# Output products of a gated linear recurrence: one layout against another, ahead of a folded feed-forward part on one Trainium2 core

## The chip, the cores and the metric

The kernel runs on one core of one Trainium2 chip. The metric is device time in microseconds of that core for one execution, the median over several runs. Engines are named as the profile names them: PE is TensorE (PEld its weight loads), DVE is VectorE, ACT is ScalarE, POOL is GpSimd, SP is the engine that issues most DMAs.

## What is computed

The reference has two parts. A recurrence with a state per batch and head, decayed per feature by alpha, is read by q at each step; then a feed-forward part takes, element by element, the largest of three products, and multiplies it by a last matrix.

```
B, H, S, D = 4, 8, 768, 48
for t in range(S):
    state = alpha[:, :, t, :, None] * state + einsum('bhd,bhe->bhde', k[:, :, t], v[:, :, t])
    y[:, :, t] = einsum('bhd,bhde->bhe', q[:, :, t], state)
x = y.transpose(0, 2, 1, 3).reshape(B * S, H * D)          # 3072 x 384
h = maximum(maximum(x @ w1, x @ w2), x @ w3)               # 3072 x 768
out = h @ w_out                                            # 3072 x 384, float32
```

## The kernel before

Tokens are cut into 24 units: 6 blocks of 128 steps (cb) times 4 batches (b), unit u = 4 cb + b. Within a unit the recurrence is written as products. ACT takes the logarithm of alpha (L398), PE sums it along time with a triangular matrix (`cums`, L438), and ACT makes the two exponentials `ep` and `en` (L443, L446). DVE or POOL multiplies them into q and k (L450). The values v are scaled on POOL or ACT with a factor per row, `vsc` (L457, L460), into tiles of 384 columns, one stretch of 48 per head. The scaled q and k are turned by PE and copied out (L479, L486), or, for the units in `CROSS_Q`, turned by a DMA. Then `scores` (L495) makes for each of 8 heads a 128 x 128 product of k and q; these use 48 rows, two heads of a pair in the upper and the lower half of the array. DVE masks them into `LA` (L500).

`output(u)` makes the unit's outputs. In `outs` (L538, L541) the stationary operands are the turned q of a head pair (against the state Z of that pair, 96 columns) and the masked scores LA of one head (against 48 columns of v). The result has steps in partitions and features in columns. `left` copies it out of PSUM into `xb` with the factor per row `ysc` that takes back the scaling of v (L552 on ACT, L554 on DVE). Since the feed-forward part needs features in partitions, `turn` (L568) turns `xb` with 3 PE transposes and a second copy makes `xT` (L573); for the three units in `CROSS_X` a DMA turns it instead (L561). Units 0 to 3 have no state yet, so their `outs` has only the 8 products with v.

`state(u)` makes the next state: PE's `sums` (L600), DVE's addition `U` (L607), and two multiplications by the decay G on POOL or DVE (`Z`, L613). The state tiles hold 4 pairs of 96 columns.

`ffn` takes one unit at a time (the first four and the last two) or two. In `grow` (L638) it multiplies xT by the differences w2 - w1 and w3 - w1, in `relu` and `max` (L649, L654) it takes the largest with zero, and in `shrink` (L674) it multiplies this by w_out and adds xT times the product w1 w_out, which `turned` and `folded` make once (L362, L379). `ob` copies the result out (L689), and `store` writes it.

The order of all work is written out by hand: every piece is a step with a number, `ORDER` lists the numbers in the order in which they are issued to their engines, `BANKS` gives each PSUM result one of 8 banks, and `PICK` names the steps that take the second of their engines. The durations in `plan.step` are those by which the order was once made; at run time they do nothing. `warm` puts 27 products of zeros (L582) into PE's stream in the first stage.

The setup clears parts of tiles: `la`, `qk` and all of Z, on DVE (L274, L276, L279).

Of the kernel before, what the change touches and what calls it, by code (L numbers as in the profile page):

```python
# [16 lines left out]
CDEC = 0.92  # L17
SIG = 128.0

# [9 lines left out]
CROSS_X = (16, 20, 22)  # L29
# [50 lines left out]
)  # L80
BANKS = (
# [9 lines left out]
)  # L91
PICK = {
# [8 lines left out]
}  # L101

# [68 lines left out]
def kernel(  # L171
# [103 lines left out]
    for t in qks[:QKS]:  # L275
        nc.vector.memset(t[:, :, :, D:], 0.0)  # L276
# [486 lines left out]
```

## Time and profile before

| | |
|---|---|
| median of three runs | 153.33 us |
| lowest and highest run | 152.72 and 155.74 us |
| span of the profiled execution | 466.5 us |
| PE busy in it | 457.5 us |
| DVE, ACT, POOL busy | 112.5, 90.1, 48.0 us |
| read from memory, written | 23.69 MB, 4.72 MB |

The profiled execution has no time of its own beside its span; the span runs from the first to the last instruction. It is three times the median of the timed runs, so a number of the trace can't be carried over to them without a look at what in it is slow; the prediction does that first.

How to read the lines: the head of the page gives each engine's busy time, its share of the span and its number of instructions. A line of the groups names the line of the kernel, the engine, the operation, output and inputs, their shapes and the number of instructions; then busy time and the mean duration of one in ns; then the idle time of the engine ahead of them and who ended it. A line of the timeline gives start and duration in us, then the same names; neighbours of one kind are merged, and x6 is their number. The duration of a matmul is modelled, its start is recorded, so distances between starts are the safer measure.

### The profile page before, as it was taken

What the parts mean: (1) busy time and instruction counts of PE and PEld (TensorE: products, weight loads), DVE (VectorE), ACT (ScalarE), POOL (GpSimd) and SP (SyncE); (2) the same over time, 40 slices, a digit from 0 to 9 for tenths busy, and PEclk for the clock granted to TensorE, in tenths of its full rate; (3) what the DMA queues carried; (4) which work ended last, traced back from release to release, by engine and by line L of the source; (5) the groups of instructions that cost most, each with busy time, mean ns of one, the idle gap of its engine ahead of it and who ended that gap; (6) DMA issues with size and microseconds to landing.
All of it is one profiled execution on the core that took longest, in us unless ns stands there. A gap on an engine that the chain in (4) does not pass through costs nothing.

```text
span 466.5 us, 4171 instructions
## 1 busy us (share of the span) xinstructions
PE 457.5 (98%) x1683; PEld 263.5 (56%) x1683; DVE 112.5 (24%) x196; ACT 90.1 (19%) x177; POOL 48.0 (10%) x72
## 2 busy tenths in 40 slices
PE   4999999999999999999999999999999999999997
PEld 1667556674555656547546645545546554567473
DVE  5420313131123122222412221322221321231100
ACT  4323221122121312111212200121220111001010
POOL 0110002003001030210111120011110020000000
DMA  9999500540087000700032640020550030100001
GB/s 179 272 287 209 110 0 1 111 76 1 0 163 124 1 0 18 152 17 35 0 60 49 141 91 9 2 62 0 112 112 17 18 79 25 35 0 25 1 34 34
DMA packets 116131, 31.07 MB, mean 67 GB/s; under 512 B 109712, under 2 KB 114960, under 8 KB 116112
## 3 DMA queue, kind: packets, MB, share of 16 engines
q1 hardware_dynamic: 113232, 27.27, 27.9%
q10 hardware_dynamic: 2880, 3.54, 2.2%
q8 instruction: 13, 0.21, 0.2%
q14 instruction: 6, 0.05, 0.0%
HBM read 23.69 MB, written 4.72 MB: 61 GB/s over the span
## 4 chain that ended last, share of the span: by engine, by line
PE 98%; DMA 1%; SPq 0%; DVE 0%; issue 0%; DVEq 0%
PE psum L638 38%; PE psum L674 29%; PE psum L479 6%; PE psum L495 4%; PE psum L582 4%; PE psum L541 3%; PE psum L438 3%; PE psum L568 3%; PE psum L600 3%; PE psum L538 2%; PE psum L379 2%; DMA qn<-in_q_dram 1%; PE psum L362 1%; PE psum L408 1%; SPq L304 0%; DVE qk L450 0%
## 5 line engine op out<-in xcount | busy, mean ns | idle before, releaser
L638 PE MATMUL psum<-xT,wd 128*128 128x256 f16 (+1 forms) x540 | 186.4, 602 | 0.0
L638 PEld LDWEIGHTS <-wd 128*128 128x128 f16 x540 | 105.1, 209 | 67.5 <-issue 61.5
L674 PE MATMUL psum<-wo,hT 128*128 128x384 f16 (+1 forms) x150 | 96.7, 887 | 0.0
L674 PEld LDWEIGHTS <-hT 128*128 128x128 f16 x150 | 34.4, 230 | 54.6 <-issue 52.0
L674 PE MATMUL psum<-w1o,xT 128*128 128x384 f16 (+1 forms) x75 | 50.1, 847 | 0.0
L654 DVE TENSOR_TENSOR hT<-psum,hT 128x512 f16<-128x512 f32 (+1 forms) x39 | 24.7, 647 | 99.7 <-PE psum L638 99.7
L649 ACT ACTIVATE hT<-psum 128x512 f16<-128x512 f32 (+1 forms) x39 | 21.7, 564 | 111.0 <-PE psum L638 111.0
L500 DVE TENSOR_TENSOR LA<-psum,c 128x1024 f16<-128x1024 f32 x24 | 28.9, 1221 | 41.0 <-PE psum L495 28.7
L541 PE MATMUL psum<-v,LA 128*128 128x48 f16 x192 | 30.3, 314 | 0.0
L541 PEld LDWEIGHTS <-LA 128*128 128x128 f16 x192 | 26.5, 179 | 5.7 <-issue 5.1
L613 POOL TENSOR_TENSOR Z<-U,G 48x192 f16<-48x192 f32 x26 | 14.1, 543 | 109.5 <-DVE U L607 108.5
L438 PE MATMUL psum<-la,c 128*128 128x384 f16 x24 | 19.9, 847 | 4.3 <-ACT la L398 4.3
L479 PE MATMUL psum<-c,qk 128*128 128x128 f16 x96 | 22.1, 480 | 1.7 <-DVE qk L450 1.7
L479 PEld LDWEIGHTS <-qk 128*128 128x128 f16 x96 | 16.9, 208 | 9.1 <-DVE qk L450 4.0
L450 POOL TENSOR_TENSOR qk<-qn,ep 128x384 f16<-128x384 f32 x11 | 10.9, 994 | 105.2 <-ACT ep L443 94.0
L674 PEld LDWEIGHTS <-xT 128*128 128x128 f16 x75 | 13.1, 185 | 14.7 <-issue 14.2
L582 PE MATMUL psum<-Z 128*128 128x384 f16 x27 | 20.2, 869 | 0.0
L443 ACT ACTIVATE ep<-psum 128x384 f32<-128x384 f32 x24 | 11.7, 494 | 41.3 <-PE psum L438 41.2
L689 ACT COPY ob<-psum 128x384 f32<-128x384 f32 (+1 forms) x18 | 8.3, 469 | 54.7 <-PE psum L674 54.7
L554 DVE TENSOR_SCALAR xb<-psum,c 128x384 f16<-128x384 f32 x15 | 9.2, 617 | 37.9 <-PE psum L541 37.9
L568 PE MATMUL psum<-c,xb 128*128 128x128 f16 x63 | 17.5, 455 | 0.0
L446 ACT ACTIVATE en<-psum 128x384 f32<-128x384 f32 x24 | 11.5, 490 | 28.4 <-PE psum L438 27.1
(61 smaller groups left out, 297.2 us busy)
## 6 DMA issues: line engine op xcount, KB each, us to landing
out_dram<-ob ACTq DMA_DIRECT2D x17, 192.0 KB, 1.9
an<-in_alpha_dram SPq DMA_DIRECT2D x8, 384.0 KB, 5.3
kn<-in_k_dram SPq DMA_DIRECT2D x8, 384.0 KB, 5.4
qn<-in_q_dram SPq DMA_DIRECT2D x8, 384.0 KB, 5.7
vn<-in_v_dram SPq DMA_DIRECT2D x8, 384.0 KB, 4.2
ws<-in_moe_w_dram SPq DMA_DIRECT2D x3, 768.0 KB, 6.7
an<-in_alpha_dram SPq DMA_DIRECT2D x8, 192.0 KB, 4.0
kn<-in_k_dram SPq DMA_DIRECT2D x8, 192.0 KB, 4.0
```

The costliest lines, as they stand in the source:

```text
L438: nc.tensor.matmul(live[Lk], tri, la[:, hs, :D], start=True, stop=True)
L479: nc.tensor.transpose(live[tk][:, w, j, :], qk[:, w, 2 * j:2 * j + 2, :], ident)
L495: nc.tensor.matmul(live[Ak][:, p, j * P:(j + 1) * P], qkT[rows, 1, j, :], qkT[rows, 0, j, :], start=True, stop=True)
L500: lambda e: nc.vector.tensor_mul(LA.rearrange("p a b t -> p (a b) t"), live[Ak].rearrange("p a (b t) -> p (a b) t", t=P), maskA.unsqueeze( ...
L541: nc.tensor.matmul(yp[:, 2 * j + p, :], LA[:, p, j, :], v16[:, 2 * j + p, :], start=(cb == 0), stop=True, skip_group_check=True)
L568: nc.tensor.transpose(live[xk][:, ft, :], xb[:, ft * P:(ft + 1) * P], ident)
L582: nc.tensor.matmul(live["wm"], zero[:, :P], zero, start=True, stop=True)
L613: lambda e, rows=rows, cols=cols: engines[e].tensor_mul(Zn[rows, :, cols], (Us[u % 3] if cb else live[pk])[rows, :, cols], G[rows, i * NP: ...
L638: nc.tensor.matmul(live[gk][:, jj, :], wd[:, kt, g, j * P:(j + 1) * P], xT[:, kt, :], start=(kt == 0), stop=(kt == NFT - 1))
L649: lambda e, h=h, gk=gk: nc.scalar.activation(out=h, in_=live[gk], func=AFT.Relu),
L654: lambda e, h=h, gk=gk: nc.vector.tensor_max(h, live[gk], h),
L674: nc.tensor.matmul(live[ok][:, cols], a[:, i * P:(i + 1) * P], w[:, cols], start=(kt == 0), stop=(kt == nk - 1))
```

## The change

The 64 features of each half of a 128-feature block of xT are now made directly, features in partitions and steps in columns. Values and state become the stationary operands, 64 columns of them at a time, and LA and the turned q the moving ones, 128 columns each. Heads are 48 wide, so a 64-feature half takes columns of two neighbouring heads; that a head adds nothing to its neighbour's features, v is stored twice as wide (768 columns), even heads in the first 384 and odd heads in the second, zeros elsewhere, and the state likewise in tiles of 512 columns, with pairs 0 and 2 at one offset and 1 and 3 at another. The two halves of a block go to PSUM partitions 0 to 63 and 64 to 127 of the same columns, and their products are issued alternately. `xb`, its turn, the second copy and the three DMA turns are gone; the first copy writes xT, with the constant factor 1/16. The factor per row moves to `ob`, where steps are in partitions again. `ORDER` is the old one without the steps that are gone, with the steps `xT` where `xb` stood; `BANKS` and `PICK` follow. The v tiles are cleared on POOL at the start.

```
+XS = 1.0 / 16.0
-CROSS_X = (16, 20, 22)
+    ZP = P + HALF // 2
-        [SIG / dec, dec / SIG, np.full(P, HALF * np.log(CDEC))], axis=1
+        [SIG / dec, dec / SIG / XS, np.full(P, HALF * np.log(CDEC))], axis=1
-    v16s = homes(7, [P, H, D], FP16, "v")
+    v16s = homes(7, [P, 2 * DM], FP16, "v")
-    Zs = [homes(B, [P, NP, 2 * D], FP16, f"Z{i}_") for i in range(2)]
+    Zs = [homes(B, [P, NP * P], FP16, f"Z{i}_") for i in range(2)]
+    def heads_of(t):
+        return bass.AP(t.tensor, t.offset, [t.ap[0], [DM + D, 2], [2 * D, NP], [1, D]])
+    def pairs_of(t):
+        return bass.AP(t.tensor, t.offset, [t.ap[0], [2 * P, NP // 2], [ZP, 2], [1, 2 * D]])
+    for t in v16s:
+        nc.gpsimd.memset(t, 0.0)
+        def terms(g):
+            lo, hi = g * HALF, (g + 1) * HALF
+            out = []
+            if cb > 0:
+                for j in range(NP):
+                    if 2 * D * j < hi and 2 * D * (j + 1) > lo:
+                        at = (j // 2) * 2 * P + (j % 2) * ZP + lo - 2 * D * j
+                        out.append((Z[:, at:at + HALF], qkT[:, 0, j, :]))
+            for h in range(H):
+                if D * h < hi and D * (h + 1) > lo:
+                    at = (h % 2) * DM + lo
+                    out.append((v16[:, at:at + HALF], LA[:, h % 2, h // 2, :]))
+            return out
         def outs(e):
-            yp = live[yk] = bank(yk, [P, H, D], FP32)
-            for j in range(NP):
-                if cb > 0:
-                    nc.tensor.matmul(yp[:, 2 * j:2 * j + 2, :], qkT[:, 0, j, :], Z[:, j, :], ...)
-                for p in range(2):
-                    nc.tensor.matmul(yp[:, 2 * j + p, :], LA[:, p, j, :], v16[:, 2 * j + p, :], ...)
+            yp = live[yk] = bank(yk, [P, NFT, P], FP32)
+            for i in range(NFT):
+                both = [terms(2 * i), terms(2 * i + 1)]
+                for k in range(max(map(len, both))):
+                    for w in range(2):
+                        if k < len(both[w]):
+                            lhsT, rhs = both[w][k]
+                            nc.tensor.matmul(yp[w * HALF:(w + 1) * HALF, i, :], lhsT, rhs,
+                                             start=(k == 0), stop=(k == len(both[w]) - 1),
+                                             skip_group_check=True)
         def left(e):
-            (ACT or DVE) xb = y * ysc
+            (ACT or DVE) xT = live[yk] * XS
-        def turn(e): ...
-        plan.step(f"x turn {u}", ...), plan.step(f"xT {u}", ...)
...
-                              nc.scalar.copy if e == "ACT" else nc.vector.tensor_copy)(
-                                  out=ob, in_=live[ok][:, cols]),
+                              nc.scalar.activation(out=ob, in_=live[ok][:, cols], func=AFT.Copy,
+                                                   scale=ysc) if e == "ACT" else
+                              nc.vector.tensor_scalar(out=ob, in0=live[ok][:, cols], scalar1=ysc,
+                                                      scalar2=None, op0=AOP.mult)),
```

The writes of v, and the reads and writes of the state in `U`, `Z` and `sums`, go through `heads_of` and `pairs_of`; their number of elements is the same.

More of the change, by code (lines that the diff above doesn't have):

```diff
@@ L239 @@
     qks = homes(QKS, [P, 2, H, DP], FP16, "qk")
-    v16s = homes(7, [P, H, D], FP16, "v")
+    v16s = homes(7, [P, 2 * DM], FP16, "v")
     qkTs = homes(QKTS, [P, 2, NP, P], FP16, "qkT")
     LAs = homes(3, [P, 2, NP, P], FP16, "LA")
-    xbs = homes(5, [P, DM], FP16, "xb")
     xTs = homes(NX, [P, NFT, B * P], FP16, "xT")
@@ L453, in prep @@
                       writes=[("qk", hq[u], w)])
+        vin = ld["v"][n % LOADED][:, hs].rearrange("p (m y) d -> p y m d", y=2)
         def scaled(e):
             if e == "ACT":
-                nc.scalar.activation(out=v16, in_=ld["v"][n % LOADED][:, hs], func=AFT.Copy,
-                                     scale=vsc)
-            else:
-                nc.gpsimd.tensor_scalar(out=v16, in0=ld["v"][n % LOADED][:, hs], scalar1=vsc,
-                                        scalar2=1.0, op0=AOP.mult, op1=AOP.mult)
+                nc.scalar.activation(out=heads_of(v16), in_=vin, func=AFT.Copy, scale=vsc)
+            else:
+                nc.gpsimd.tensor_scalar(out=heads_of(v16), in0=vin, scalar1=vsc, scalar2=1.0,
+                                        op0=AOP.mult, op1=AOP.mult)
         plan.step(f"v {u}", [("POOL", 0.59), ("ACT", 0.62)], u, scaled,
@@ L528, in output @@
         cb, b = divmod(u, B)
-        qkT, LA, v16, xb = qkTs[ht[u]], LAs[u % 3], v16s[u % 7], xbs[u % 5]
+        qkT, LA, v16 = qkTs[ht[u]], LAs[u % 3], v16s[u % 7]
         Z = Zs[cb % 2][b]
-        yk, xk = ("yp", u), ("xp", u)
+        yk = ("yp", u)
         xT = xTs[cb % NX][:, :, b * P:(b + 1) * P]
-        def outs(e):
-            yp = live[yk] = bank(yk, [P, H, D], FP32)
-            for j in range(NP):
-                if cb > 0:
-                    nc.tensor.matmul(yp[:, 2 * j:2 * j + 2, :], qkT[:, 0, j, :], Z[:, j, :],
-                                     start=True, stop=False, skip_group_check=True)
-                for p in range(2):
-                    nc.tensor.matmul(yp[:, 2 * j + p, :], LA[:, p, j, :], v16[:, 2 * j + p, :],
-                                     start=(cb == 0), stop=True, skip_group_check=True)
-        plan.step(f"outs {u}", [("PE", 0.374 if cb else 0.21)], u, outs, banks=[yk], writes=[yk],
+        def terms(g):
[11 more added lines that the diff above has]
+            return out
+        def outs(e):
+            yp = live[yk] = bank(yk, [P, NFT, P], FP32)
[8 more added lines that the diff above has]
+                                             skip_group_check=True)
+        plan.step(f"outs {u}", [("PE", 0.55 if cb else 0.33)], u, outs, banks=[yk], writes=[yk],
                   reads=[("qkT", ht[u]), ("LA", u % 3), ("v16", u % 7), ("qkT room", ht[u]),
@@ L549, in left @@
         def left(e):
-            y = live[yk].rearrange("p a b -> p (a b)")
             if e == "ACT":
-                nc.scalar.activation(out=xb, in_=y, func=AFT.Copy, scale=ysc)
+                nc.scalar.activation(out=xT, in_=live[yk], func=AFT.Copy, scale=XS)
             else:
-                nc.vector.tensor_scalar(out=xb, in0=y, scalar1=ysc, scalar2=1.0, op0=AOP.mult,
-                                        op1=AOP.mult)
-        plan.step(f"xb {u}", [("ACT", 0.58), ("DVE", 0.56)], u, left, reads=[yk],
-                  writes=[("xb", u % 5)])
-        if u in CROSS_X:
-            plan.step(f"cross x {u}", cross_options(0.55), u - 2.0,
-                      lambda e: nc.sync.dma_start_transpose(out=xT, in_=xb),
-                      reads=[("xb", u % 5)], writes=[("xT", cb % NX, b)])
-            return
-        def turn(e):
-            live[xk] = bank(xk, [P, NFT, P], FP16)
-            for ft in range(NFT):
-                nc.tensor.transpose(live[xk][:, ft, :], xb[:, ft * P:(ft + 1) * P], ident)
-        plan.step(f"x turn {u}", [("PE", 0.167)], u, turn, banks=[xk], reads=[("xb", u % 5)],
-                  writes=[xk])
-        plan.step(f"xT {u}", [("DVE", 0.35), ("ACT", 0.5)], u,
-                  lambda e: (nc.vector.tensor_copy if e == "DVE" else nc.scalar.copy)(
-                      out=xT, in_=live[xk]),
-                  reads=[xk], writes=[("xT", cb % NX, b)])
+                nc.vector.tensor_scalar(out=xT, in0=live[yk], scalar1=XS, scalar2=None,
+                                        op0=AOP.mult)
+        plan.step(f"xT {u}", [("ACT", 0.58), ("DVE", 0.56)], u, left, reads=[yk],
+                  writes=[("xT", cb % NX, b)])
     def warm(u, w, count):
-        zero = Zs[1][0].rearrange("p a b -> p (a b)")
+        zero = Zs[1][0][:, :DM]
         def zeros(e):
@@ L600, in sums @@
                 nc.tensor.matmul(live[pk][:, j, :], qk[:, 1, 2 * j:2 * j + 2, :],
-                                 v16[:, 2 * j:2 * j + 2, :], start=True, stop=True)
+                                 heads_of(v16)[:, :, j, :], start=True, stop=True)
         plan.step(f"sums {u}", [("PE", 0.17)], u + 2, sums, banks=[pk],
@@ L606, in state @@
             plan.step(f"U {u}", [("DVE", 0.55)], u + 2,
-                      lambda e: nc.vector.tensor_add(Us[u % 3], live[pk], Z),
+                      lambda e: nc.vector.tensor_add(
+                          Us[u % 3].rearrange("p (a b) x -> p a b x", b=2),
+                          live[pk].rearrange("p (a b) x -> p a b x", b=2), pairs_of(Z)),
                       reads=[pk, ("Z", cb % 2, b)], writes=[("U", u % 3)])
@@ L613, in state @@
                       lambda e, rows=rows, cols=cols: engines[e].tensor_mul(
-                          Zn[rows, :, cols], (Us[u % 3] if cb else live[pk])[rows, :, cols],
-                          G[rows, i * NP:(i + 1) * NP].unsqueeze(2).broadcast_to([D, NP, D])),
+                          pairs_of(Zn)[rows, :, :, cols],
+                          (Us[u % 3] if cb else live[pk])[rows, :, cols].rearrange(
+                              "p (a b) x -> p a b x", b=2),
+                          G[rows, i * NP:(i + 1) * NP].rearrange("p (a b) -> p a b", b=2)
+                          .unsqueeze(3).broadcast_to([D, NP // 2, 2, D])),
                       reads=[("U", u % 3) if cb else pk, ("G", n % 3)],
```

117 rows, old and new, of tables (BANKS, ORDER, PICK) are left out of this document.

## The prediction

> **What bounds the kernel now.** I read the page's head first, then one window of busy times, then TensorE's timeline at single matmuls, since the head leaves a riddle: the profiled execution spans 466.5 us, and the three timed runs have a median of 153.33 us.
>
> ```profile
> span 466.5 us, 4171 instructions
> PE 457.5 (98%) x1683; PEld 263.5 (56%) x1683; DVE 112.5 (24%) x196; ACT 90.1 (19%) x177; POOL 48.0 (10%) x72
> PE 98%; DMA 1%; SPq 0%; DVE 0%; issue 0%; DVEq 0%
> 33.00:462.90 429.90, 429.90 (x1556) 248.12 (x1555) 97.33 (x160) 77.59 (x157) 44.05 (x64) 1.00 0.25 52
> ```
>
> The last line is the window from the first product of the feed-forward part to the last copy out: busy time of PE, PEld, DVE, ACT, POOL, then the clock column, DMA share and GB/s. TensorE has no idle time in it at all. The clock column says 1.00, but single products (from the timeline: start, duration, form) say otherwise:
>
> ```profile
> 200.91 0.74 PE L638 MATMUL psum<-xT,wd 128*128 128x256 f16 x1
> 203.01 2.06 PE L674 MATMUL psum<-w1o,xT 128*128 128x384 f16 x3
> 204.74 4.10 PE L674 MATMUL psum<-wo,hT 128*128 128x384 f16 x6
> 208.52 2.68 PE L638 MATMUL psum<-xT,wd 128*128 128x256 f16 x6
> 212.31 0.37 PE L479 MATMUL psum<-c,qk 128*128 128x128 f16 x1
> 212.37 0.73 PE L479 MATMUL psum<-c,qk 128*128 128x128 f16 x2
> 423.34 0.35 PE L538 MATMUL psum<-Z,qkT 128*128 128x96 f16 x1
> 423.38 0.36 PE L541 MATMUL psum<-v,LA 128*128 128x48 f16 x2
> 211.27 0.33 PE L541 MATMUL psum<-v,LA 128*128 128x48 f16 x1
> 211.29 0.35 PE L538 MATMUL psum<-Z,ws 128*128 128x96 f16 x1
> ```
>
> Six products of 384 columns take 208.52 - 204.74 = 3.78 us from start to start, 0.63 us each, so 128 columns take 0.21 us. Single pairs of starts lie far closer: 0.06 us for 128 columns, 0.04 for 96, 0.02 for 48. The array passes work in bursts at about four times its mean pace, and stands off between. A quarter of 0.21 is 0.0525 us for 128 columns, which those bursts confirm. So I read the profile as one at quarter pace, and the timed runs as ones at full pace: 429.9 / 4 = 107.5 us, plus the 33.0 us ahead of the window and 3.6 us behind it, is 144 us, near 153.33. The remaining 9 us holds what a quarter-pace profile cannot show (waits of a fast TensorE, and what lies around the span). So at full pace TensorE still sets the time from about 33 us on, but DVE (97.3 us of some 108 to 117) has little slack. Everything below is costed at both paces; the forecast is for the timed runs.
>
> **Part 1: output products and turn.** Before, a unit with state has 4 products of 96 columns (L538) and 8 of 48 (L541), and, unless its unit is in CROSS_X, 3 turns of 128 (L568).
>
> ```profile
> 210.89 0.52 PE L538 MATMUL psum<-Z,ws 128*128 128x96 f16 x1
> 212.31 1.83 PE L479 MATMUL psum<-c,qk 128*128 128x128 f16 x8
> 421.92 0.95 PE L568 MATMUL psum<-c,xb 128*128 128x128 f16 x3
> 422.55 0.51 PE L538 MATMUL psum<-Z,qkT 128*128 128x96 f16 x1
> 199.06 1.75 PE L495 MATMUL psum<-ws 48*128 48x128 f16 x16
> 200.74 2.43 PE L638 MATMUL psum<-xT,wd 128*128 128x256 f16 x6
> ```
>
> At quarter pace the block takes 212.31 - 210.89 = 1.42 us and the turn 422.55 - 421.92 = 0.63, together 2.05. After: each of six 64-feature halves gets 2 heads and 1 or 2 head pairs, 20 products of 128 columns (12 without state), issued in turn into the two column halves of the array. The trace has no column halves, but it has row halves: 16 score products of 128 columns take 200.74 - 199.06 = 1.68 us, 0.21 per two, so the two of a pair run wholly side by side. I take the same for column halves: 10 pairs, 2.10 us at quarter pace, 10 x 0.0525 = 0.53 at full pace. The two halves get 10 products each, so no half is left over.
>
> Before at full pace: 4 x 0.04 + 8 x 0.025 + 3 x 0.0525 = 0.52 us (0.025 is the 0.02 shown, rounded up, since starts are given to 0.01). So 17 units gain nothing (+0.01 each, +0.2), and the three CROSS_X units, whose turn was a DMA, pay 0.53 - 0.36 = +0.17 each, +0.5. Three of the four units without state lie here, among products of zeros (L582) that only fill time, and the fourth has 6 pairs, 0.32 us, for 0.36:
>
> ```profile
> 19.51 0.95 PE L541 MATMUL psum<-v,LA 128*128 128x48 f16 x8
> 23.76 0.95 PE L541 MATMUL psum<-v,LA 128*128 128x48 f16 x8
> 24.55 0.79 PE L582 MATMUL psum<-Z 128*128 128x384 f16 x1
> 30.54 2.84 PE L582 MATMUL psum<-Z 128*128 128x384 f16 x4
> ```
>
> Streams: **+0.7 us**. At quarter pace: 17 x 0.05 + 3 x 0.68 = +2.9.
>
> **Part 2: changes of array layout.** In the changed order of instructions the output blocks stand alone among full-array work, 24 blocks, so 24 entries and 24 exits are added to the 16 and 16 around the scores. What one costs is seen beside scores:
>
> ```profile
> 230.52 0.38 PE L495 MATMUL psum<-qkT 48*128 48x128 f16 x2
> 230.83 0.70 PE L568 MATMUL psum<-c,xb 128*128 128x128 f16 x3
> 200.28 0.53 PE L495 MATMUL psum<-ws 48*128 48x128 f16 x2
> ```
>
> After the last pair the next product should start 0.21 us on. It starts 0.31 us on at 230.83 (0.10 late) and 0.46 on at 200.74 (0.25 late). Yet the product behind it starts at 200.91 = 200.28 + 0.21 + 0.42: nothing is lost in the end, because an array that stands off three quarters of the time has room for it. At full pace that cover is gone. Bounds for one change: 0 (the net at quarter pace) and 0.25 us (the later start); nothing excludes 0, and a gain is excluded, since a change never lets a product start early. I take 0.10, the least late start, as the row least mixed with standing off. Units 0 to 2 lie among the zeros, so 42 of 48 count: **+4.2 us** (0 to 10.5).
>
> The Trainium skill, page "TensorEngine Tiling (Array Packing)", section "Key Properties", says that changing the tiling mode, not just the tile, drains TensorE; the late starts agree, the quarter-pace sum shows no net loss, and the rule gives no figure. By that rule the term stands above 0, and the sum stays as it is.
>
> **Part 3: copies out, and what waits for them.**
>
> ```profile
> L554 DVE TENSOR_SCALAR xb<-psum,c 128x384 f16<-128x384 f32 x15 | 9.2, 617 | 37.9 <-PE psum L541 37.9
> L573 DVE COPY xT<-psum 128x384 f16<-128x384 f16 x14 | 4.8, 356 | 38.9 <-PE psum L568 38.8
> L552 ACT ACTIVATE xb<-psum,c 128x384 f16<-128x384 f32 x9 | 5.2, 581 | 53.3 <-PE psum L541 53.3
> L573 ACT COPY xT<-psum 128x384 f16<-128x384 f16 x7 | 3.3, 477 | 23.7 <-PE psum L568 23.7
> L689 ACT COPY ob<-psum 128x384 f32<-128x384 f32 x17 | 8.0, 478 | 48.7 <-PE psum L674 48.7
> ```
>
> The first copies stay (15 on DVE, 9 on ACT, same engines, now writing xT); the second ones go: 14 x 0.356 = 5.0 us of DVE, 7 x 0.477 = 3.3 us of ACT. The decay factor moves into the 18 ACT copies of the result: a factor per partition costs at most 581 - 478 = 0.10 us, 1.8 us of ACT, and 0.10 us at the very end. No PE wait for a second copy can arise any more, and three DMA transposes leave SP's queue. What this is worth at full pace the trace does not show (in it TensorE never waits there): between 0 and what is left of the 9 us, less 32 existing changes x 0.10 = 3.2, so 0 to 5.8. Before, the order already puts other products between a block and its turn, so I take a small part: **-0.7 us**.
>
> **Part 4: the rest.** Seven POOL clears of v (768 elements a partition) lie ahead of its first product:
>
> ```profile
> L345 POOL MEMSET ws<- 128x256 f16 x4 | 1.1, 312 | 19.2 <-DVE wd L337 19.2
> 11.58 1.00 POOL L450 TENSOR_TENSOR qk<-qn,ep 128x384 f16<-128x384 f32 x1 [11.14 <-DMA qn<-in_q_dram]
> 2.53 1.67 DVE L279 MEMSET Z<- 128x192 uint32 x8
> 5.91 0.56 DVE L450 TENSOR_TENSOR qk<-qn,ep 128x384 f16<-128x384 f32 x1 [1.71 <-DMA qn<-in_q_dram]
> ```
>
> At 3 x 0.312 each they end near 0.4 + 6.6 = 7 us, 4.5 us before POOL's first work; without that cover they would cost 6.6 us. Z grows from 192 to 256 words, 1.67 to 2.2 us, inside 1.71 us in which DVE waits for q. Strided views of v, Z and U hold the same 384 elements in runs of 48 and more: 0. SP keeps its loads in order, with three issues fewer.
>
> **Sum.** Timed runs: 153.33 + 0.7 + 4.2 - 0.7 = **157.5 us**. The profiled execution, if again at quarter pace: 466.5 + 2.9, about 469 us, 3.0 times the timed figure as now.
>
> **Rivals.** *Free changes of layout:* the net of 0 seen at quarter pace holds at full pace too. For it speaks the start at 200.91; against it that this cover is the standing off. Then 153.33 + 0.7 - 0.7 = 153.3, no change. *The copies were the limit (the other side):* DVE, busy for 97.3 of some 117 us, delays the turned x often; with 5.0 us off DVE and the wait gone nearly all 5.8 us return, and with free changes that gives 153.33 + 0.7 - 5.8 = 148.2. It decides once the relief passes 3.8 us more than the changes cost; against it, TensorE's own work already explains 144 us. *Halves not side by side:* a product's weights are loaded right ahead of it, and if loading into one half stops the other, 20 products take 20 x 0.0525 = 1.05 us a block, +0.525 x 20 = 10.5, so 168; with half of that, 163. For it: each product has a load of its own, 20 instead of 12 + 3; against it: the row halves overlap perfectly, with as many loads.
>
> The same page of the Trainium skill, section "Tile-to-Partition Mapping", says that column tiling disables the fast weight load. No run here shows it; by it the third rival would be the likelier the slower a 64-column load is.
>
> **Chances.** Forecast 0.50; free changes 0.20; copies were the limit 0.14; halves not side by side 0.16. Two per cent is about what a measurement of this kernel can tell from no change: 150.3 to 156.4 us. The forecast's own range is 154.5 to 161 (changes at 0.04 to 0.18 us); 0.45 of its 0.50 lies above 156.4. So slower 0.45 + 0.16 = 0.61, same 0.05 + 0.20 = 0.25, faster 0.14. The range reaches down into the copies' case (149.5) and up to half of the third rival (163.5), leaving out somewhat under 1 in 10 at either end.
>
> **What would show it.** The page's pace tells first which execution it is: 0.21 or 0.0525 us for 128 columns. Right: a block of 20 products lasts about ten times the pace of one product, products of the two halves start together, and at full pace the product before and after a block is some 0.1 us late. Free changes: full-pace neighbours start on time. Third rival: a block lasts 15 to 20 paces. The second: at full pace TensorE before shows waits on xT or xb that are absent after. The sum fails outright if POOL's clears reach past 11.6 us, or if xT's copies fall behind, since the next product of the feed-forward part stands right behind a block on TensorE.

## The result, and the profile after

| | before | after |
|---|---|---|
| median of the first comparison | 153.33 us, 3 runs (152.72 to 155.74) | 156.99 us, 3 runs (156.92 to 157.18) |
| ratio, with its 95% interval | | 1.027 [1.021, 1.034] |
| median of a repeat on another chip | 152.0 us, 11 runs | 156.33 us, 6 runs |
| ratio of the repeat | | 1.028 [1.023, 1.034] |
| span of a profile at full pace | 149.7 us | 155.2 and 154.6 us |

The changed kernel is slower by 2.7%: 157.0 us, where 157.5 was forecast. Its profile came at full pace, unlike the profile of before that the prediction had to work from. So the kernel before was profiled once more, and that execution, at full pace too, is the one compared here. First the head of the page of the changed kernel: engines, the DMA engines in tenths over 40 slices, and the shares of the chain that ended last.

```profile
span 155.2 us, 4373 instructions
PE 140.6 (91%) x1796; PEld 105.3 (68%) x1796; DVE 105.7 (68%) x182; ACT 86.2 (56%) x170; POOL 54.9 (35%) x79
...
DMA  6998999999989999999999999989999899121032
...
PE 80%; SPq 9%; DMA 4%; DVE 2%; ACT 1%; issue 1%; DVEq 0%
```

The same lines of the kernel before, at full pace:

```profile
span 149.7 us, 4171 instructions
PE 134.9 (90%) x1683; PEld 105.2 (70%) x1683; DVE 109.3 (73%) x196; ACT 88.1 (59%) x177; POOL 49.5 (33%) x72
...
DMA  5999999979989999999899999999999999832032
...
PE 67%; DMA 13%; SPq 11%; ACT 4%; issue 2%; DVE 1%; ACTq 0%; DVEq 0%
```

Two things are to be seen. TensorE is busy for 5.7 us more, with 113 more matmuls, and the span grows by 5.5 us: the loss lies on TensorE. And before, 13% of the chain was DMA, now 4% (7% in a second profile of the changed kernel): before, TensorE at times waited for transfers, and the slower one waits for them less. The DMA engines are at nine tenths or more in almost every slice up to about 130 us, in both. That last fact the prediction did not use, and it decides most of what follows.

Now one output block. TensorE's timeline of the changed kernel, start and duration:

```profile
86.97 0.71 PE L643 MATMUL psum<-xT,wd 128*128 128x256 f16 x5
87.61 0.25 PE L558 MATMUL psum<-qkT,Z 128*64 128x128 f16 x2
87.69 0.22 PE L558 MATMUL psum<-LA,v 128*64 128x128 f16 x1
87.69 0.22 PE L558 MATMUL psum<-qkT,Z 128*64 128x128 f16 x1
...
88.29 0.35 PE L409 MATMUL psum<-c,la 128*128 128x2 f16 x8
```

The same place in the kernel before, and, a little earlier, a turn:

```profile
83.79 0.71 PE L638 MATMUL psum<-xT,wd 128*128 128x256 f16 x5
84.33 0.21 PE L538 MATMUL psum<-Z,qkT 128*128 128x96 f16 x1
...
84.71 0.34 PE L408 MATMUL psum<-c,la 128*128 128x2 f16 x8
```

```profile
77.13 0.33 PE L568 MATMUL psum<-c,xb 128*128 128x128 f16 x3
77.30 0.21 PE L538 MATMUL psum<-Z,ws 128*128 128x96 f16 x1
```

Before, five feed-forward products reach to the block in 0.54 us, after in 0.64: 0.1 us late. The block then takes 0.38 us before (0.374 in finer starts) and 0.68 after (0.682), from its first start to the next product's. That 0.68 is ten pairs 0.056 us apart, the first pair some 0.024 longer, and the next product again 0.096 late. Both products of a pair start together (87.69 and 87.69). Counting the late entry, a block takes 0.776 us in place of 0.374 and of a turn of 0.167.

The copies out, from the groups of the changed kernel (mean ns behind the comma), stand as predicted or better:

```profile
L571 DVE TENSOR_SCALAR xT<-psum 128x384 f16<-128x384 f32 x15 | 8.2, 555 | 8.5 <-PE psum L558 8.5
L569 ACT ACTIVATE xT<-psum 128x384 f16<-128x384 f32 x9 | 4.4, 490 | 14.5 <-PE psum L558 12.7
L695 ACT ACTIVATE ob<-psum,c 128x384 f32<-128x384 f32 x17 | 9.8, 579 | 8.3 <-PE psum L679 8.3
```

With a constant factor the first copies cost 555 in place of 617 ns on DVE (where a second multiplication, by 1.0, went too) and 490 in place of 581 on ACT; the late factor makes the copies of the result dearer by the 0.10 us expected.

### The profile page after: what moved, and what is told of

Same layout as the page of the kernel before. It is cut to its first block, busy times and chain, and to the rows that moved or that the text cites. A ratio compares the mean times of both kernels' runs of the same rounds, so it can differ in the third digit from the quotient of the medians.

```text
span 155.2 us, 4373 instructions
## 1 busy us (share of the span) xinstructions
PE 140.6 (91%) x1796; PEld 105.3 (68%) x1796; DVE 105.7 (68%) x182; ACT 86.2 (56%) x170; POOL 54.9 (35%) x79
## 4 chain that ended last, share of the span: by engine, by line
PE 80%; SPq 9%; DMA 4%; DVE 2%; ACT 1%; issue 1%; DVEq 0%
PE psum L643 32%; PE psum L679 23%; PE psum L558 9%; SPq L305 8%; PE psum L497 4%; PE psum L481 4%; DMA ws<-in_moe_w_dram 4%; PE psum L439 3%; PE psum L600 2%; PE psum L380 2%; PE psum L409 1%; DVE wd L338 1%; SPq L324 1%; DVE ob L697 1%; PE psum L582 1%
## 5 line engine op out<-in xcount | busy, mean ns | idle before, releaser
L643 PE MATMUL psum<-xT,wd 128*128 128x256 f16 (+1 forms) x540 | 54.6, 251 | 1.4 <-DVE wd L338 0.7
L643 PEld LDWEIGHTS <-wd 128*128 128x128 f16 x540 | 42.7, 98 | 8.0 <-DVE wd L338 1.1
L679 PE MATMUL psum<-wo,hT 128*128 128x384 f16 (+1 forms) x150 | 27.7, 320 | 0.0
L679 PEld LDWEIGHTS <-hT 128*128 128x128 f16 x150 | 14.5, 98 | 8.9
L679 PE MATMUL psum<-w1o,xT 128*128 128x384 f16 (+1 forms) x75 | 15.8, 320 | 0.4 <-DVE ob L697 0.4
L558 PE MATMUL psum<-LA,v 128*64 128x128 f16 x288 | 16.1, 227 | 0.0
L558 PEld LDWEIGHTS <-v 128*64 128x64 f16 x288 | 13.1, 114 | 1.2 <-issue 0.9
L399 ACT ACTIVATE la<-an 128x384 f16<-128x384 f32 (+1 forms) x16 | 10.9, 687 | 4.2 <-DMA an<-in_alpha_dram 4.2
L439 PE MATMUL psum<-la,c 128*128 128x384 f16 x24 | 8.0, 350 | 4.5 <-ACT la L399 4.5
L481 PE MATMUL psum<-c,qk 128*128 128x128 f16 x96 | 8.8, 242 | 3.3 <-DVE qk L451 2.7
```

The lines of the kernel that those rows point to most:

```text
L439: nc.tensor.matmul(live[Lk], tri, la[:, hs, :D], start=True, stop=True)
L481: nc.tensor.transpose(live[tk][:, w, j, :], qk[:, w, 2 * j:2 * j + 2, :], ident)
L558: nc.tensor.matmul(yp[w * HALF:(w + 1) * HALF, i, :], lhsT, rhs, start=(k == 0), stop=(k == len(both[w]) - 1), skip_group_check=True)
L643: nc.tensor.matmul(live[gk][:, jj, :], wd[:, kt, g, j * P:(j + 1) * P], xT[:, kt, :], start=(kt == 0), stop=(kt == NFT - 1))
L679: nc.tensor.matmul(live[ok][:, cols], a[:, i * P:(i + 1) * P], w[:, cols], start=(kt == 0), stop=(kt == nk - 1))
```

## The experiments

**The changed kernel again**, unaltered, on another chip.

> The changed kernel again, as the measure for the next kernel on the same chip. Both theories: 157.0 us, 1.02 to 1.03 of the kernel before.

Measured: 156.33 us, against 152.0 for the kernel before on the same chip. The result holds. Its trace shows the same late starts; from the first product of the feed-forward part to TensorE's last product it takes 126.75 us, the first profile 127.64, the kernel before 123.4. So +3.8 us, the mean of the two, lie in this main stage.

**The kernel before, profiled at full pace**, unaltered.

> The kernel before, unchanged, for a profile at full pace. Theory (changes of array layout cost 0.095 us each, and about 2 us come back from waits for the turn): 128 columns take 0.056 us, a block of output products 0.36 to 0.38 us, a turn 0.165 to 0.17 us, no late start at a block, and TensorE waits about 2 us in all after 35 us of the span that the changed kernel does not have. Rival (the relief is nothing, and the old block is dearer than the bursts of the quarter-pace trace said): no such waits, and block and turn together take 0.60 us or more instead of 0.53.

Measured: 151.5 us, and the profile shown above. 128 columns take 0.056 us (0.0525 forecast from a quarter of 0.21), and the first product of the feed-forward part starts at 22.60 us, not at 33. A block and a turn take 0.374 + 0.167 = 0.54 us, as the theory had it, and not the 0.60 of its rival. The waits of TensorE in this execution, which the quarter-pace profile could not show, are next (us in total, times, the longest), without those of the first 20 us; the last two are for DMA turns:

```profile
...
PE psum L638 <- ACT hT L649: 1.3, 1, 1.3
PE psum L638 <- DVE wd L337: 0.6, 1, 0.6
PE psum L495 <- DMA qkT<-qk: 0.6, 1, 0.6
...
PE psum L495 <- DMA ws<-qk: 0.5, 1, 0.5
```

In the changed kernel's list no DMA turn appears, and no wait for hT:

```profile
...
PE psum L643 <- DVE wd L338: 0.7, 1, 0.7
PE psum L643 <- ACT w1T L369: 0.7, 1, 0.7
```

In both, TensorE waits 0.5 us for one copy of qkT as well. Neither list holds a wait on xT or xb, so in these executions the second copies were not the limit.

**The changes of layout alone.** The kernel before, with one tiny product of 64 stationary and 2 moving columns ahead of each of the 24 blocks: an entry and an exit each, and no other work.

```
+            nc.tensor.matmul(psall[:HALF, place[yk], DM:DM + 2], ident[:, :HALF], hsel,
+                             start=True, stop=True, skip_group_check=True)
```

> The kernel before, with one tiny product added ahead of each of the 24 output blocks: 64 stationary columns, 2 moving ones, into unused PSUM columns. So only changes of array layout are added, 24 into the column halves and 24 out of them; the result is not touched. Theory (a change costs 0.095 us): 21 blocks behind the start pay 0.19 us and some 0.025 us for the product, +4.5 us, about 157.8 us. Rival (changes cost nothing; the new products or the layouts of v and Z are what costs): 21 x 0.025, +0.5 us, about 153.9 us.

Measured: 155.27 us, ratio 1.022 [1.017, 1.027]. Both expected times were reckoned from 153.33 us, and the kernel before took 152.0 on this chip; so it is the differences that compare: +3.3 us, where the theory had +4.5 and free changes +0.5. It is clearly more than free changes allow, yet short of the theory. The timeline of this kernel shows why both:

```profile
86.41 0.60 PE L640 MATMUL psum<-xT,wd 128*128 128x256 f16 x4
86.94 0.19 PE L536 MATMUL psum<-c 128*64 128x2 f16 x1
87.07 0.22 PE L540 MATMUL psum<-Z,qkT 128*128 128x96 f16 x1
...
87.45 0.29 PE L408 MATMUL psum<-c,la 128*128 128x2 f16 x6
```

Four products of 256 columns should take 0.44 us and the tiny one starts after 0.53; its neighbour starts 0.12 behind it (0.123), where such tiny products in the whole array (L408) stand 0.025 apart. Per block TensorE needs 0.227 us more than before, over 21 blocks 4.8 us. The main stage grew by 3.9 in the trace and the median by 3.3. The rest of the 4.8 is in the waits: behind the first product of the feed-forward part they sum to 2.9 us before and 2.0 here. Those for hT (1.3) and for DMA turns (0.6 and 0.5) are gone, and one of 0.9 for a copy of the result is new. So a change of layout costs what was forecast, and a part of it is paid out of waits. By itself this refutes free changes.

**Fewer changes.** The changed kernel with work at eight places moved in `ORDER`, so that two output blocks, or a block and scores, stand together there; 65 of 80 changes are left. The diff shows one of the places.

```
-    330, 168, 331, 169, 336, 205, 180, 207, ...
+    330, 205, 331, 168, 169, 336, 180, 207, ...
...
```

> The changed kernel with TensorE's order moved a little: work between two neighbouring output blocks is put ahead of them, so that 65 changes of layout are left of 80; products and copies are the same. Theory: 15 x 0.095 = 1.4 us less than the changed kernel, about 155.6 us. Rival (changes cost nothing): 157.0 us, or a little more where the moved work waits.

Measured: 155.64 us, ratio 1.026 [1.021, 1.031]; 0.7 us under the unaltered changed kernel, where 15 changes at 0.094 are worth 1.4. The intervals of the two ratios overlap, so this difference of the medians is not clear of noise; the traces say more. The late starts behind the first product of the feed-forward part sum to 4.9 us in place of 6.3, so TensorE got the 1.4 back. But its waits in this stretch sum to 2.1 us, where the two profiles of the unaltered kernel have 1.6 and 0.7. One of them is on a line that the other order lacked:

```profile
PE psum L437 <- DVE LA L500: 0.7, 1, 0.7
...
```

In these profiles an order that suits the array suits the other engines less: some two thirds of the saving went to waits. The price of a change holds; what the order saves in the end is not settled by these runs.

**Order of the halves.** The changed kernel, with all products of one half issued before those of the other.

```
-                for k in range(max(map(len, both))):
-                    for w in range(2):
+                for w in range(2):
+                    for k in range(max(map(len, both))):
```

> The changed kernel with the products of a 128-feature block issued half by half (all of the lower half, then all of the upper) in place of alternately; same products, same changes of layout. Theory (the halves run side by side only where neighbours in the order lie in different halves): a block grows from 0.68 to some 1.0 us, since about 7 of 10 overlaps go; 20 x 0.35 = 7 us slower than the changed kernel, about 163 us. Rival (the order of the halves is of no account): 156.3 us.

Measured: 156.43 us, as the unaltered changed kernel; the theory's 163 is missed by far. The block in this kernel's timeline:

```profile
65.73 0.25 PE L558 MATMUL psum<-ws,Z 128*64 128x128 f16 x2
...
66.42 0.39 PE L643 MATMUL psum<-xT,wd 128*128 128x256 f16 x2
```

It takes 66.42 - 65.73 = 0.69 us as before. Either the halves run side by side whatever the order within three or four products, or a product with 64 columns of weights takes half the time and nothing runs side by side at all. The next kernel separates these.

**All products in one half.** The changed kernel with all 20 products of a block written to partitions 0 to 63; those of the other half are not written.

```
-  nc.tensor.matmul(yp[w * HALF:(w + 1) * HALF, i, :], lhsT, rhs, start=(k == 0), ...
+  nc.tensor.matmul(yp[:HALF, i, :], lhsT, rhs, start=(k == 0 and w == 0), ...
```

> The changed kernel with all 20 products of a block sent to the lower column half (partitions 0 to 63; the upper half is left as it was, so half of the features are not made). Theory A (two products share the array only when they lie in different halves): a block takes 20 x 0.056 = 1.1 us in place of 0.68, some 9 us more. Theory B (after the run with halves in turn: a product of half width passes in half the time by itself): the block stays at 0.68 us and the time at 156 us.

Measured, in one run: 166.12 us, about 10 us above the changed kernel. Its block:

```profile
66.98 0.30 PE L558 MATMUL psum<-ws,Z 128*64 128x128 f16 x2
67.12 0.22 PE L558 MATMUL psum<-LA,v 128*64 128x128 f16 x1
67.17 0.22 PE L558 MATMUL psum<-ws,Z 128*64 128x128 f16 x1
...
68.22 0.39 PE L643 MATMUL psum<-xT,wd 128*128 128x256 f16 x2
```

68.22 - 66.98 = 1.24 us, with starts 0.056 apart. So a single product of 64 columns costs as much as a full one, and the halves do run side by side in the changed kernel.

**No turn.** The kernel before without its turns, second copies and DMA turns; the first copy writes xT, unturned (on DVE as on ACT).

```
-                nc.scalar.activation(out=xb, in_=y, func=AFT.Copy, scale=ysc)
+                nc.scalar.activation(out=xT, in_=y, func=AFT.Copy, scale=ysc)
...
-                      lambda e: nc.sync.dma_start_transpose(out=xT, in_=xb),
+                      lambda e: None,
...
-                nc.tensor.transpose(live[xk][:, ft, :], xb[:, ft * P:(ft + 1) * P], ident)
+            pass
```

> The kernel before with the turn left out: the first copy writes xT straight away, the PE transposes, the second copies and the three DMA turns are not issued, so the features reach the feed-forward part unturned. It prices what the change saves. The turn is 0.167 us of TensorE at full pace, 18 of them behind the start: 3.0 us. Theory (beyond that about 1.5 us of waits go with the copies and the DMAs): about 147.5 us against 152.0. Rival one (the copies and DMAs were hidden): 149.0 us. Rival two (the copies were the limit): 146 us or less.

Measured: 150.25 us in 12 runs, ratio 0.993 [0.989, 0.998]. That misses every one of the expected times: TensorE loses 3.0 us of work, DVE and ACT their second copies, and the time falls by 1.0 to 1.8 us (the ratio's 0.7%, and the difference of the medians). The waits of this kernel:

```profile
PE psum L635 <- DVE wd L337: 1.2, 1, 1.2
PE psum L635 <- POOL wd L337: 1.1, 1, 1.1
PE psum L495 <- DMA ws<-qk: 0.8, 2, 0.5
...
PE psum L495 <- DMA qkT<-qk: 0.6, 1, 0.6
PE psum L495 <- DMA qkT<-ws: 0.5, 1, 0.5
```

TensorE now waits 1.9 us for DMA turns of q and k, 1.1 before, and 2.3 for the weights wd, 0.6 before. A new theory: transfers pace the kernel before as well, so work taken off TensorE turns into waiting for them. The kernels with fewer transfers, at the end, test it.

**The late factor alone.** The kernel before, with the factor per row moved from the first copies to `ob`, on DVE as on ACT.

```
-                nc.scalar.activation(out=xb, in_=y, func=AFT.Copy, scale=ysc)
+                nc.scalar.activation(out=xb, in_=y, func=AFT.Copy, scale=XS)
...
-                              nc.scalar.copy if e == "ACT" else nc.vector.tensor_copy)(
+                              nc.scalar.activation(..., scale=ysc) if e == "ACT" else
```

> The kernel before with only the late factor: the first copy takes the constant 1/16, the last copy takes the factor per row. Theory: first copies get about 0.06 (DVE) and 0.09 us (ACT) shorter, last copies 0.09 us longer, none of it on TensorE's path but 0.09 us at the very end: 152.0 us, within 0.5. Rival (the last copies hold up the stores and the banks): a microsecond or more slower.

Measured: 153.11 us in 6 runs, ratio 1.013 [1.007, 1.018], so 1.1 us above the 152.0 of the theory, which missed; the rival had a microsecond or more. Its profile shows one place that the other kernels lack:

```profile
92.69 0.62 PE L496 MATMUL psum<-qkT 48*128 48x128 f16 x16 [1.76 <-DMA qkT<-qk]
95.13 2.08 PE L674 MATMUL psum<-wo,hT 128*128 128x384 f16 x6
```

The first line is a wait of 1.76 us for a DMA turn; in the second, six products of 384 columns take 2.08 us where they take 1.14 at full pace. The window around the second tells why, by its clock column, the third number from the end:

```profile
94.00:96.00 2.00, 2.00 (x8) 1.02 (x7) 2.00 (x3) 1.08 (x2) 1.15 (x2) 0.50 1.37 234
```

The granted clock was 0.50 there, and 1.00 again from 98 us on. That is not what makes this kernel slower: three of its runs, with a mean clock of 1.00, took 152.3 to 153.6 us as well. Whether the wait stands in every run is not known, and why a later factor should make a turn late was not tried. So the cause of the 1.1 us stays open, and with it how much of it the changed kernel pays. Its two profiles have 0.4 us and nothing of waits of TensorE for copies of the result, and the next experiment puts a loose bound on it.

**The old products on the new layouts.** The changed kernel with the old 96- and 48-column products, unturned, reading the wide v and Z; clears, late factor, `ORDER` and copies are the changed kernel's.

```
+            for j in range(NP):
+                if cb > 0:
+                    at = (j // 2) * 2 * P + (j % 2) * ZP
+                    nc.tensor.matmul(yp[:, 2 * j:2 * j + 2, :], qkT[:, 0, j, :], Z[:, at:at + 2 * D], ...)
+                for p in range(2):
+                    at = p * DM + (2 * j + p) * D
+                    nc.tensor.matmul(yp[:, 2 * j + p, :], LA[:, p, j, :], v16[:, at:at + D], ...)
```

> The changed kernel with the old form of output products: turned q and masked scores stationary, 96 and 48 columns moving, all in the full array, from the new layouts of v and Z; the result is not turned. Everything else of the change is in it. Theory (the products and their changes of layout are the cost): 20 blocks lose 0.40 us and one 0.35, 8.4 us less than the changed kernel, about 148 us, and the first product of the feed-forward part moves back from 23.6 to about 22.6 us of the span. Rival (the clears of v, the wider Z or the strided views cost too): 149.5 us or more, and the first such product stays at 23.6 us.

Measured: 150.92 us in 12 runs, ratio 0.997 [0.993, 1.002]. By its time the rival won, by the start of the feed-forward part the theory: its first product starts at 22.5 us, in the first profile of the changed kernel at 23.62. Neither is borne out in full. The kernel without a turn has none of the clears, layouts and the late factor, and is only 0.7 us faster, with overlapping intervals; so these together cost little, and what the theory missed is the waiting that comes when TensorE has less to do. And the start varies in the changed form by itself (below). The products of the new form are worth 156.3 - 150.9 = 5.4 us, though TensorE has 8.4 us less to do (0.776 - 0.374 = 0.40 for each of 21 blocks).

**Fewer transfers.** Three kernels leave out the eight later loads of q of 384 KB each, so that some units reuse old values of q: the kernel before, the one without a turn, and the changed one.

```
- engines[e].dma_start(
+ x == "q" and n >= LOADED or engines[e].dma_start(
```

> The kernel before with the eight later loads of q (384 KB each) left out, so that later units use old q: 3.1 of 23.7 MB less to read, one in four of the loads that come after the start; all engine work stays. It asks whether transfers pace the kernel before. Theory (the DMA engines, busy 9 tenths and more to about 127 us, hold TensorE up a little): 150 to 151 us against 152.0. Rival (transfers are hidden): 152.0 us.

> The kernel before without turn, second copies and DMA turns (the features stay unturned), and without the eight later loads of q. Theory (without the turn the transfers paced it, and ate two thirds of the saving): with fewer loads the whole saving of some 3 us shows, 3 us under the kernel before with fewer loads, about 147.5 us. Rival (what ate the saving is the order of the steps and the waits between engines): again only 1 to 1.5 us under that kernel, 149 us or more.

> The changed kernel without the eight later loads of q. Theory (its TensorE is slow enough that transfers no longer matter): within 0.7 us of the changed kernel, 155.6 to 156.4 us. Rival (transfers pace it as well): as much faster as the kernel before gets.

Measured, beside 152.02 us for the kernel before on the same chip: 149.92 us, ratio 0.987 [0.982, 0.992]; 147.77, ratio 0.975 [0.969, 0.980]; 156.22, ratio 1.029 [1.024, 1.034]. The loads are worth 2.1 us to the kernel before, and nothing to the changed one (156.33 with them on another chip). This contrast is clear of noise. Dropping the turn saves 149.92 - 147.77 = 2.15 us without these loads, and 1.0 to 1.8 with them, of 3.0; this smaller difference is within the scatter of the runs. One stretch of four kernels shows how it comes: busy time of PE, PEld, DVE, ACT, POOL with their numbers, clock, DMA share (it can come out a little above 1) and GB/s. First before, then without a turn:

```profile
110.00:135.00 25.00, 24.45 (x304) 19.28 (x300) 20.82 (x35) 12.61 (x27) 9.13 (x14) 1.00 0.95 184
```

```profile
110.00:135.00 25.00, 23.36 (x295) 18.36 (x294) 19.20 (x31) 12.44 (x27) 8.58 (x13) 1.00 0.94 179
```

Then without a turn and with fewer loads, and the changed kernel with all loads:

```profile
110.00:135.00 25.00, 25.00 (x322) 20.61 (x320) 20.30 (x32) 12.30 (x26) 7.51 (x12) 1.00 0.69 139
```

```profile
110.00:135.00 25.00, 25.00 (x331) 18.40 (x328) 18.75 (x32) 12.92 (x28) 9.37 (x14) 1.00 1.01 186
```

With the DMA engines at 0.95 TensorE idles for 0.55 us of 25, and with less work for 1.64. With the DMA engines at 0.69 it is busy all the time. The share alone does not decide it: from 35 to 60 us it is 1.05 before, and TensorE has no idle time. What it waits for in the stretch shown are DMA turns, 0.5 us before and 1.3 us without a turn. The theory holds in its direction; 0.85 us of the 3.0 still do not come back, and where they go was not traced.

## Why the prediction was right, and where a step was off

The time, the sign and the main cause were right: slower by changes of layout. The rest was not small, but nearly cancelled. Step by step:

- **The pace.** The profile of before was at a quarter of full pace, as read. The full-pace profile has 0.056 us for 128 columns. The make-up of the 153.33 us was read wrong: the feed-forward part begins at 22.6 us, not 33.0, and its stage takes 123.4 us up to TensorE's last product, where a quarter of the old window, which ran on to the last copy out, gave 107.5.
- **Changes of layout, +4.2 forecast.** 0.094 each against 0.10, 42 x 0.094 = 3.95 us. Late starts at every block and the kernel with changes alone show it. The rows around scores were the right proxy: in the full-pace profile of before, a start into scores is 0.096 us late and one out of them 0.094 (medians), for blocks of the changed kernel 0.093 and 0.097. That of the two late starts on record, 0.10 and 0.25, the smaller was the one to take was argued, not shown. The Trainium skill, page "TensorEngine Tiling (Array Packing)", section "Key Properties", has TensorE drain on a change of tiling mode; the 0.09 us on either side of a block agree with that.
- **Streams, +0.7 forecast, +1.4 measured.** The whole block path costs 17 x (0.776 - 0.374 - 0.167) = 4.0, three former CROSS_X units 3 x (0.776 - 0.374) = 1.2, and the last unit without state 0.2, in sum 5.4; less 3.95 for changes that leaves 1.4. A pair takes 0.056 and not 0.0525, and the first 0.024 more.
- **Relief, -0.7 forecast, -1.6 measured.** Of 5.4 us of added work the main stage grew by 3.8. What went are not waits on copies, as the prediction had it. Behind the first feed-forward product TensorE waits for 2.9 us in all before, so most of the 9 us out of which the relief was to come were TensorE's own time; in the changed kernel it waits for 1.6 and 0.7. The waits for DMA turns of q and k went: the four profiled kernels with the old products, all loads and nothing added have 1.1, 1.9, 1.8 and 1.6 us of them, the six with blocks or tiny products in half of the array and all loads have none, and neither have the three with fewer loads. That fits transfers which arrive in time once TensorE is slower, or loads are fewer. The wait of 1.3 us for hT went too, but it is in only one profile of the old form, and a wait of 1.1 for hT is in one of the new; it may be scatter. Here the mechanism was wrong as well as the size.
- **The start, 0 forecast, -0.2 to +1.3 measured.** The first feed-forward product starts at 23.62 and 23.93 us in the two profiles of the changed kernel, against 22.60. Over all six profiles with the new products it varies from 22.36 to 23.93, with a mean of 23.13; over the seven with the old ones it stays between 22.48 and 22.73. The forecast's reason was that the first blocks lie among zeros and so cost nothing. They are dearer, with pairs half as fast as later: in the timeline of TensorE in the changed kernel the first block takes 0.78 us to the next product,

```profile
17.41 0.85 PE L558 MATMUL psum<-LA,v 128*64 128x128 f16 x12
18.19 1.14 PE L582 MATMUL psum<-Z 128*128 128x384 f16 x3
```

and before 0.36:

```profile
16.68 0.52 PE L541 MATMUL psum<-v,LA 128*128 128x48 f16 x8
17.04 1.14 PE L582 MATMUL psum<-Z 128*128 128x384 f16 x3
```

But the first block also starts 0.73 us later, ahead of any new product: ACT makes `w1h`, for which TensorE waits there, at 15.13 in place of 14.54 us, when a load has come. The feed-forward part then waits for DVE's subtraction wd, and DVE copies the result of a block ahead of it. In the timeline of DVE in the changed kernel:

```profile
21.02 0.56 DVE L571 TENSOR_SCALAR xT<-psum 128x384 f16<-128x384 f32 x1 [2.16 <-PE psum L558]
21.80 1.76 DVE L338 TENSOR_TENSOR wd<-ws,w1h 128x1536 f16<-128x1536 f32 x1 [0.22 <-DMA ws<-in_moe_w_dram]
```

Before, the subtraction starts 1.0 us earlier:

```profile
20.78 1.76 DVE L337 TENSOR_TENSOR wd<-ws,w1h 128x1536 f16<-128x1536 f32 x1 [0.68 <-DMA ws<-in_moe_w_dram]
```

In both it waits last for a load of weights (0.22 and 0.68 us). In the second profile of the changed kernel the copy ends last, at 22.2 us. And in the changed kernel with fewer loads, with the same first blocks, the subtraction starts no later than before, at 20.69 us, and the feed-forward part at 22.50:

```profile
20.22 0.56 DVE L571 TENSOR_SCALAR xT<-psum 128x384 f16<-128x384 f32 x1 [2.21 <-PE psum L558]
20.69 1.75 DVE L338 TENSOR_TENSOR wd<-ws,w1h 128x1536 f16<-128x1536 f32 x1
```

So the dearer first blocks can hide behind the load, and where the start was late, late loads had a part in it. The load for the subtraction landed at 21.2 to 21.7 us in four of the six profiles, and at 20.4 to 20.8 in the other two and in all seven of the old form. How much of the mean +0.5 us is the loads', and why they came late, stays open.

- **POOL's clears, 0 forecast.** They end at 5.5 us, where 7 was put, ahead of POOL's first work, and cost nothing.

```profile
0.73 4.78 POOL L277 MEMSET v<- 128x768 f16 x7 [0.29 <-POOLq L754]
```

- **The end.** Behind the last product 3.9 us in place of 3.7, the late factor and spread.

The sum of the traces: 3.8 + 1.2 + 0.2 = 5.2 us, the mean of the spans' 4.9 and 5.5; with the mean start, +0.5, it is 4.5, and the medians differ by 3.7 and 4.3. The forecast's +4.2 was so near partly by chance: twice the streams and a later start were balanced by twice the relief. A slip in the range: changes at 0.04 us each give 155.0 us, not its lower end of 154.5.

The rivals. *Free changes* fell by the late starts and by the kernel with changes alone. *The copies were the limit* fell by the kernel without a turn: with all copies and turns gone and nothing added it was faster by 0.7%, where the rival wanted 5 us. *Halves not side by side* fell by the pairs that start together, and its price was right: with one half alone the block costs 1.24 us, 10 us in all, where 10.5 were put. The Trainium skill, page "TensorEngine Tiling (Array Packing)", section "Tile-to-Partition Mapping", says that column tiling disables the fast weight load. The trace shows no cost of that beyond, at most, the 0.024 us of the first pair: the others are 0.056 us apart, a full product's own pace.

No kernel run here beats both with all of the work done. Of the changed form, with all loads, the one with fewer changes has the lowest median, 155.64 us, not clear of noise.

## What to carry to other kernels

Count how often TensorE changes between whole-array and part-array products: here each change cost 0.094 us, more than a pair of 128-column products, so a short block of part-array products can lose more at its two edges than it saves inside. Before you promise what less TensorE work will bring, look at the DMA row of the page: at nine tenths, added TensorE work was charged at about 70%, and of work taken away a third to two thirds came back. And see whether the profile was taken at the pace of the timed runs before you scale it.

## What of the hardware was not expected

- A whole execution ran at a quarter of TensorE's pace: 466.5 us of span beside 153.33 us timed. The clock column said 1.00, but the page of that execution has no row for the granted clock, which the pages at full pace have; so the 1.00 was no reading.
- The two column halves need not be fed in turn. With one half's three or four products issued ahead of the other's, a block took 0.69 us, as with alternating ones; with one half alone 1.24.
- A copy of 128x384 out of PSUM with a constant factor is cheaper than with one per partition: 490 against 581 ns on ACT, 555 against 617 on DVE. On DVE the dropped second multiplication is not the reason as far as `ob` shows: its plain copy takes 553 ns, and one multiplication by a factor per partition 613.
- Entering and leaving the row halves of the scores and the column halves of the blocks costs alike, in the median 0.093 to 0.097 us each way.
